# Column stores on GpSimd's queue, gates on ScalarE, and the tokens' places scattered in the last stage

## The chip, the cores and the metric

The kernel runs on one core of a Trainium2 chip. The metric is the device time of one execution in microseconds, given as the median of several runs.

## The reference

Three stages follow each other on 3072 tokens of width 512: chunked attention (8 heads, chunks of 32 with a few neighbours and 8 memory keys), a mixture of 8 experts where each token goes to the one expert with the largest logit, and a dense block with a rational activation.

```python
e_idx = np.argmax(logits, axis=1)              # one expert for each token
for e in range(E):
    mask = e_idx == e
    h = np.maximum(x[mask] @ w1[e], 0.0)       # 512 -> 1024
    out[mask] = gate_w[mask, None] * (h @ w2[e])
...
h = x @ w_in                                   # 512 -> 2048, all tokens
P = a[0] + a[1]*h + a[2]*h2 + a[3]*h3
Q = 1.0 + abs(b[0])*abs(h) + abs(b[1])*h2
return ((P / (Q + 1e-06)) @ w_out)
```

All in float32; the kernel multiplies float32 numbers as two rounded halves (high and low), which gives three products for each.

## The kernel before, in words

One program runs on the five engines, and every engine works through its own instructions in the order in which the code is written. SyncE (SP) and GpSimd (POOL) also issue DMAs, each in order on a queue of its own.

**Attention** fills the first 110 us or so, writes the rows `x` to DRAM (`xd`), and a router sorts the tokens by expert into units of 128 slots. There are 32 units (`NS`): 0 to 2 early ones, 3 to 22 in five quads of four units (`QUADS`), 23 a single last one (`S_LAST`), 24 to 29 for overflow, and 30 and 31 two small ones of at most 32 tokens. A unit's tokens belong to one expert; empty slots have an index out of bounds, which a DMA skips.

**The experts' stage** is `moe`, with the nested `quad(q)`. A quad has 8 steps `n`, of 128 hidden features each. `mm1_quad(n)` makes 12 matmuls of 512 columns (`hq`), `relu_quad(n)` cuts them on ScalarE into `hh` (line 1025) and on VectorE into `hl` (line 1026), and `mm2_quad(n - 1)` makes 12 matmuls into four accumulators (`pb`, `pa`). Behind that, `at(n)` does the work at the side:

- `filler()` is one step of the converter of the dense block's weights, which arrive as 64-bit floats: cast a piece to high and low (lines 1324, 1325; of `w_out` the halves also go out to `wod` in DRAM by GpSimd, lines 1327, 1328), load the piece after the next on SP (512 KB, line 1311, tile `wr`), and turn the bits of the next one, first on ScalarE (line 1262, which reads the loaded piece), then on VectorE (lines 1263 to 1266).
- `load_w` loads the next quad's expert weights on SP, 1 MB in a step, where the expert changes; `split_w` cuts them into high and low on ScalarE and VectorE (lines 917, 920).
- `gather` fetches the next quad's rows of `x` (four indirect DMAs of 128 rows on GpSimd, line 807), and `gate_x` multiplies each unit by its gate on GpSimd (line 907).
- `put_row(s)` scatters, for unit s, each token's number to its place in `od` (an indirect DMA on GpSimd of 128 words of 4 bytes, line 897). Quads 0 to 3 do it at every step, so unit s goes out at quad s // 8, step s % 8.

At a quad's end `put_quad` copies the four accumulators out (ScalarE and VectorE in turn) and stores them to `yd`, 256 KB each, on SP's queue (line 984). `prep_x` transposes the next quad's gathered units on TensorE (line 1081, tile `xps`): units 0 and 1 at step 7, units 2 and 3 behind the loop. Quads 0 and 3 carry a small unit as well (`mm1_small`, line 856, reads `w1r`).

Behind the last quad come the single unit's ReLU (line 1071), the turning of its hidden features (`prep_h`, lines 939 to 942), the first block's `rows.prep` (lines 1288, 1289), and its second product (line 949).

**The dense stage** is `moe2`: 6 blocks of 512 rows, 16 steps each, 24 matmuls of 512 columns a step, the second product three steps behind the first. It loads `wo` (512 KB each, from `wod`) and the next block's rows `yr` (from `yd`) on SP. `rows.load_out` reads `od` back as `out_rows` at step 4, and `evac` scatters the finished rows to the output on GpSimd (line 1472), for the first block at step 18.

Of the kernel before, what the change touches and what calls it, by code (L numbers as in the profile page):

```python
# [18 lines left out]
AF = mybir.ActivationFunctionType  # L19
ALU = mybir.AluOpType  # L20
AX = mybir.AxisListType
PSUM = bass.MemoryType.PSUM
P = 128
# [46 lines left out]
def attention(nc, tc, ex, ident, qkv, small, pos_u, out_u, start, ab):  # L70
# [8 lines left out]
    with ExitStack() as ctx:  # L79
# [190 lines left out]
        for t in range(NT):  # L270
# [13 lines left out]
            if t + NB_IN < NT + 2:  # L284
                load(t + NB_IN)
# [48 lines left out]
NS = 32  # L334
# [7 lines left out]
QUAD = 4  # L342
QUADS = 5
Q_FIRST = EARLY + 1
S_LAST = Q_FIRST + QUAD * QUADS
NC8 = 1024 // P
# [411 lines left out]
class Experts:  # L758
# [145 lines left out]

    def gate_x(self, s):
        x = self.xg[s % QUAD]
        self.nc.gpsimd.tensor_scalar(out=x, in0=x, scalar1=self.gate_s[:, s:s + 1], scalar2=None, op0=ALU.mult)

    def gate_row(self, c0, to):

# [61 lines left out]

    def put_quad(self, c0, gate=None):

        b = self.first_column(self.nc.sync, c0)
        for t in range(QUAD):
            y, ps = self.xg[(c0 + t) % QUAD], self.acc(t)
            if gate is not None:
                self.nc.vector.tensor_tensor(out=y, in0=ps, in1=gate, op=ALU.mult)
            elif t % 2 == 0:  # L980
                self.nc.scalar.copy(y, ps)
            else:
                self.nc.vector.tensor_copy(y, ps)
            self.nc.sync.dma_start(out=self.yd[t, :, bass.ds(b, QUAD * P)], in_=y)

    def clear_columns(self, zero):

# [40 lines left out]
    def acc(self, t):  # L1028
        return (*self.pb, *self.pa)[t]

    def mm2_quad(self, n):
        h, l = self.hq[n % 2]
        for t in range(QUAD):
            ps, d = self.acc(t), slice(n % 2 * 512 + t * P, n % 2 * 512 + (t + 1) * P)
            self.nc.tensor.matmul(ps, lhsT=self.w2h[:, n // 2, d], rhs=h, start=(n == 0), stop=False)
            self.nc.tensor.matmul(ps, lhsT=self.w2l[:, n // 2, d], rhs=h, start=False, stop=False)
            self.nc.tensor.matmul(ps, lhsT=self.w2h[:, n // 2, d], rhs=l, start=False, stop=(n == NC8 - 1))
# [68 lines left out]
def moe(nc, tc, ex, filler, rows, gp):  # L1106
    ET = mybir.EngineType
    flags, w1r = ex.flags, ex.w1r
    gate0 = gp.tile([P, QUAD * P], F32, name="gate0")
    small = gp.tile([P, 4, SM], F32, name="small_y")  # L1110

    def quad(q):
        c0 = Q_FIRST + QUAD * q
        nxt = range(c0 + QUAD, c0 + 2 * QUAD) if q + 1 < QUADS else range(S_LAST, S_LAST + 1)
        k = QUAD_SMALL.get(q)
        pieces = {0: (1, 0), 1: (1, 2), 2: (2, 0), 3: (2, 2)}
        loads = {n if k is None else n + 4: x for n, x in pieces.items()}
        part1, part2 = (5, 6) if k is None else (6, 7)
        sx, (sh, sT) = ex.xy[3], [x[:, 0:256] for x in ex.xg[0:2]]
        sT = sT[:, 0:P].rearrange("p (k n) -> p k n", k=4)  # L1120
        hT = ex.xg[0][:, 256:512].rearrange("p (i n) -> p i n", i=2)
        if k is not None:
            e = ex.expert(NS - 1 - k)

        def at(n):

            if n in FILLERS[q]:
                filler()
            if k is not None and n in pieces:
                layer, i = pieces[n]  # L1130
                ex.load(e, layer, range(i, i + 2))
            if n in loads:
                layer, i = loads[n]
                ex.load_w(nxt[0], layer, range(i, i + 2))
            if n == part1:
                ex.split_w(nxt[0], 1, range(2))
            if n == part2:
                ex.split_w(nxt[0], 2, range(2))
            if n == (2 if k is None else 5):
                for c in nxt:  # L1140
                    ex.gather(c)
                if len(nxt) > 1:
                    for c in nxt:
                        ex.gate_x(c)
            if q < 4:
                ex.put_row(q * NC8 + n)

        for n in range(NC8):
            ps = ex.mm1_quad(n)
            if n == 0 and q == 0:  # L1150
                ex.mm2(EARLY, 0)
                ex.put(1, ex.turn(1))
                ex.mm2(EARLY, 1)
                ex.out(EARLY)
            if n == 1 and q == 0:
                ex.put(EARLY, ex.turn(EARLY))
                ex.gate_row(Q_FIRST, gate0)
            ex.relu_quad(n, ps)
            if n == 0 and q == 0:
                ex.load_w(Q_FIRST, 2)  # L1160
                ex.split_w(Q_FIRST, 2)
            if k is not None and n == 0:
                ex.gather_small(k, sx[:, 0:D_M])
            if k is not None and n == 3:
                ex.prep_x_small(sx, sT)
            if k is not None and n == 4:
                ex.prep_h_small(sh, hT)
            if k is not None and n == 5:
                ex.put_small(k, sx[:, 0:D_M], small)
            if n == NC8 - 1:  # L1170
                xs = [(c, ex.prep_x(c, c - nxt[0] if len(nxt) > 1 else None)) for c in nxt[0:2]]
                for c, low in xs:
                    low()
            if n > 0:
                ex.mm2_quad(n - 1)
            if k is not None and n == 3:
                ex.mm1_small(sT, sh)
            if k is not None and n == 4:
                ex.out_small(k, ex.mm2_small(hT), sx)
            at(n)  # L1180
        for c in nxt[2:]:
            ex.prep_x(c, c - nxt[0])()
        ex.split_w(nxt[0], 1, range(2, 4))
        if q + 1 == QUADS:
            while filler():
                pass
            rows.open()
            for t in range(4):
                rows.load(0, t, w1r[:, t, 0:TB])
            for part in range(3):  # L1190
                ex.mm1(S_LAST, part)
        ex.mm2_quad(NC8 - 1)
        ex.put_quad(c0, gate0 if q == 0 else None)
        ex.split_w(nxt[0], 2, range(2, 4))

    def first_y(t):
        rows.prep(t, w1r[:, t, 0:TB], rows.h, rows.l)

    filler()
    ex.split_w(EARLY, 2)  # L1200
    for q in range(QUADS):
        quad(q)
    ex.hs = ex.w2r[:, 0].rearrange("p (i j n) -> p i j n", i=2, j=4)
    ex.relu(S_LAST)
    for t in range(2):
        first_y(t)
    for g in range(2):
        ex.prep_h(S_LAST, g)
    for t in range(2, 4):
        first_y(t)  # L1210
    for k in range(SMALL - 1, -1, -1):
        ex.copy_small(k)
    ALL = (ET.PE, ET.Activation, ET.DVE, ET.Pool, ET.SP)
    more = nc.values_load(flags[0:1, 2, 0:1], engines=ALL, min_val=0, max_val=1)
    tc.mark_branch_hint_location("more", "LikelyTaken", engines=(ET.PE, ET.Activation))
    for g in range(2):
        ex.mm2(S_LAST, g)
    with tc.If(more == 1, label="more"):  # L1218
        ex.clear_columns(w1r[:, 0])
        for i in range(Q_FIRST, NN):  # L1220
            if i == S_LAST or i < S_LAST and (i - Q_FIRST) % QUAD == 0:
                continue
            todo = nc.values_load(flags[0:1, 2, i:i + 1], engines=ALL, min_val=0, max_val=1)
            with tc.If(todo == 1):
                e = ex.expert(i)
                for layer in (1, 2):
                    ex.load(e, layer)
                    ex.split_w(i, layer, always=True)
                nc.gpsimd.memset(ex.xg[i % QUAD], 0.0)
                ex.gather(i)  # L1230
                ex.prep_x(i)()
                for part in range(3):
                    ex.mm1(i, part)
                ex.relu(i)
                ex.prep_h(i, 0)
                ex.prep_h(i, 1)
                for part in range(2):
                    ex.mm2(i, part)
                ex.out(i)
                ex.merge(i)  # L1240
        for t in range(4):
            rows.load(0, t, w1r[:, t, 0:TB])
        for t in range(4):
            first_y(t)
    ex.out(S_LAST, y=rows.spare, ps=ex.pb[1])
# [23 lines left out]
class Rows:  # L1269
# [10 lines left out]

    def load(self, blk, k, r):
        self.nc.sync.dma_start(out=r, in_=self.ex.yd[k, :, blk * TB:(blk + 1) * TB])

    def load_out(self):
        behind(self.tc, self.nc.sync.dma_start(out=self.out, in_=self.ex.od.rearrange("(t p) a -> p (t a)", p=P)), *self.ex.outs)
# [80 lines left out]
def moe2(nc, tc, rows, wih, wil, wod, consts, out):  # L1366
    with ExitStack() as ctx:
# [114 lines left out]
        n = len(steps)  # L1482
        for i in range(n + LAG):
            if i < n:
                mm1(*steps[i])
            if i == 1:
                rows.last(hp.tile([P, NK, P], F32, tag="h", name="yps"))
            if i == 4:
                rows.load_out()
            if 1 <= i <= n:  # L1490
                ew_act2(steps[i - 1])
# [121 lines left out]
```

## Time and profile before

| what | value |
|---|---|
| runs shown | 991.28, 993.83, 1002.33 us (median 993.83) |
| profiled execution | 995.52 us, span 994.0 us |
| PE busy | 931.9 us (94%), mean granted clock 0.974 |
| DVE, ACT, POOL busy | 747.1, 535.5, 166.1 us |
| attention, experts, dense block | about 0 to 115, 115 to 460, 460 to 994 us |

The span is the time between the first and the last instruction of the profiled execution; 1.5 us lie outside it. PE counts as busy while matmuls stream, also at half clock, so its share says where it had work and not how fast it went.

### The profile page before, as it was taken

The numbers are of one execution on the slowest core, as the hardware profiler recorded it, in microseconds if no ns is written. First come the engines' busy times: TensorE is split into PE (matmuls) and PEld (weight loads), VectorE is DVE, ScalarE is ACT, GpSimd is POOL, SyncE is SP. The second block draws the span as 40 slices with busy tenths as digits, with TensorE's granted clock in tenths as the row PEclk, the third lists the DMA queues.
The fourth block names the chain that finished last, engine by engine and source line by source line (L and its number), as shares of the span: only waits on it lengthen the run. The fifth ranks groups of instructions, "written<-read, shape, count | busy, mean of one in ns | idle before, by whom it ended". The sixth has DMA issues, their size and how long they took to land.

```text
span 994.0 us, 15359 instructions
## 1 busy us (share of the span) xinstructions
PE 931.9 (94%) x5684; PEld 752.5 (76%) x5684; DVE 747.1 (75%) x1244; ACT 535.5 (54%) x897; POOL 166.1 (17%) x194
## 2 busy tenths in 40 slices
PE   6998899797888798998999999999999999999997
PEld 5676578585667677887788888888888888888885
DVE  7677783284384725644999989998998999899885
ACT  3453433231161613324777767667776766777673
POOL 5112203074323127310000100010010001001001
PEclk9999899898889799999999999999999999999999
DMA  8998535769839365855421100010010001001001
GB/s 333 350 372 320 199 109 77 163 150 229 132 110 250 106 236 165 260 182 184 154 89 39 43 12 22 11 43 22 22 43 11 22 11 43 22 1 44 1 1 43
DMA packets 39093, 114.89 MB, mean 116 GB/s; under 512 B 8987, under 2 KB 9119, under 8 KB 36192
## 3 DMA queue, kind: packets, MB, share of 16 engines
q1 hardware_dynamic: 28800, 84.31, 29.1%
q0 software_dynamic: 9888, 28.60, 8.7%
q8 instruction: 46, 0.75, 0.3%
q10 hardware_dynamic: 320, 0.91, 0.3%
q14 instruction: 39, 0.32, 0.1%
HBM read 86.51 MB, written 27.54 MB: 115 GB/s over the span
## 4 chain that ended last, share of the span: by engine, by line
issue 57%; PE 17%; DMA 15%; POOL 5%; DVE 4%; ACT 1%; SPq 1%; POOLq 0%; ACTq 0%; DVEq 0%
DMA wod<-wo 3%; DMA wr<-in_moe_w_in 3%; DMA wr<-in_moe_w_out 2%; POOL out L1472 2%; PE pv L210 2%; DMA w1r<-in_moe_w 2%; PE pa L154 2%; PE pb L1096 1%; PE pa L949 1%; PE hq L1018 1%; PE xps L234 1%; PE hq L1019 1%; DMA out_rows<-od 1%; PE hq L1020 1%; PE pps L188 1%
## 5 line engine op out<-in xcount | busy, mean ns | idle before, releaser
L1457 PE MATMUL a<-wo,gh 128*128 128x512 f32 x384 | 149.6, 390 | 1.6 <-ACT gh L1436 1.6
L1459 PE MATMUL a<-wo,gl 128*128 128x512 f32 x384 | 149.6, 390 | 1.3 <-DVE gl L1442 1.3
L1400 PE MATMUL h<-yh,wih 128*128 128x512 f32 x384 | 149.6, 389 | 0.4 <-PEq L1218 0.4
L1402 PE MATMUL h<-yh,wil 128*128 128x512 f32 x384 | 149.4, 389 | 0.0
L1458 PE MATMUL a<-wo,gh 128*128 128x512 f32 x384 | 149.4, 389 | 0.0
L1401 PE MATMUL h<-yl,wih 128*128 128x512 f32 x384 | 149.4, 389 | 0.0
L1412 ACT ACTIVATE s<-h 128x512 f32<-128x512 f32 x96 | 56.5, 588 | 104.8 <-PE h L1402 103.0
L1472 POOL DMA_INDIRECT out<-o,out_rows x24 | 25.7, 1070 | 495.6 <-ACT o L1468 489.1
L1419 DVE SCALAR_TENSOR_TENSOR q<-s,ab,q 128x512 f32<-128x512 f32 x96 | 71.8, 748 | 40.2 <-ACT q L1413 40.2
L1459 PEld LDWEIGHTS a<-wo,gl 128*128 128x128 f32 x384 | 72.2, 188 | 17.2 <-DVE gl L1442 2.1
L1457 PEld LDWEIGHTS a<-wo,gh 128*128 128x128 f32 x384 | 72.0, 188 | 17.2 <-ACT gh L1436 2.5
L1436 ACT CAST gh<-u 128x512 fp32r<-128x512 f32 x96 | 59.9, 624 | 45.5 <-DVE u L1432 45.4
L1400 PEld LDWEIGHTS h<-yh,wih 128*128 128x128 f32 x384 | 72.1, 188 | 15.8 <-issue 0.8
L1401 PEld LDWEIGHTS h<-yl,wih 128*128 128x128 f32 x384 | 72.2, 188 | 14.9
L1458 PEld LDWEIGHTS a<-wo,gh 128*128 128x128 f32 x384 | 72.0, 187 | 15.0
L1402 PEld LDWEIGHTS h<-yh,wil 128*128 128x128 f32 x384 | 72.0, 187 | 14.9
L1414 ACT ACTIVATE u<-h,ab 128x512 f32<-128x512 f32 x96 | 74.8, 780 | 0.0
L1432 DVE SCALAR_TENSOR_TENSOR u<-u,ab,q 128x512 f32<-128x512 f32 x96 | 72.2, 752 | 3.4
L1421 DVE SCALAR_TENSOR_TENSOR u<-u,ab,h 128x512 f32<-128x512 f32 x96 | 71.8, 748 | 3.4
L1430 DVE SCALAR_TENSOR_TENSOR q<-q,ab,s 128x512 f32<-128x512 f32 x96 | 71.6, 745 | 1.7 <-ACT s L1426 1.7
L1425 ACT ACTIVATE s<-q,ab 128x512 f32<-128x512 f32 x96 | 70.2, 731 | 1.1
L1431 DVE SCALAR_TENSOR_TENSOR q<-q,s 128x512 f32<-128x512 f32 x96 | 66.4, 692 | 3.3
(307 smaller groups left out, 1817.6 us busy)
## 6 DMA issues: line engine op xcount, KB each, us to landing
in<-in_qkv SPq DMA_DIRECT2D x22, 560.0 KB
in<-in_qkv SPq DMA_DIRECT2D x22, 556.0 KB
w1r<-in_moe_w SPq DMA_DIRECT2D x20, 512.0 KB
w2r<-in_moe_w SPq DMA_DIRECT2D x20, 512.0 KB
wr<-in_moe_w_in SPq DMA_DIRECT2D x16, 512.0 KB
wr<-in_moe_w_out SPq DMA_DIRECT2D x16, 512.0 KB
wod<-wo POOLq DMA_DIRECT2D x32, 256.0 KB
wo<-wod SPq DMA_DIRECT2D x16, 512.0 KB
```

The costliest lines, as they stand in the source:

```text
L1400: nc.tensor.matmul(ps, lhsT=wih[k][:, sl], rhs=h[:, k], start=(k == 0), stop=False)
L1401: nc.tensor.matmul(ps, lhsT=wih[k][:, sl], rhs=l[:, k], start=False, stop=False)
L1402: nc.tensor.matmul(ps, lhsT=wil[k][:, sl], rhs=h[:, k], start=False, stop=(k == NK - 1))
L1414: A.activation(u, ps, func=AF.Identity, scale=a3, bias=a2)
L1419: V.scalar_tensor_tensor(out=q, in0=s, scalar=absb1, in1=q, op0=ALU.mult, op1=ALU.add)
L1421: V.scalar_tensor_tensor(out=u, in0=u, scalar=a1, in1=ps, op0=ALU.add, op1=ALU.mult)
L1425: A.activation(s, q, func=AF.Ln, bias=cb)
L1430: V.scalar_tensor_tensor(out=q, in0=q, scalar=cb, in1=s, op0=ALU.add, op1=ALU.mult)
L1432: V.scalar_tensor_tensor(out=u, in0=u, scalar=a0, in1=q, op0=ALU.add, op1=ALU.mult)
L1457: nc.tensor.matmul(ps, lhsT=gh[:, sl], rhs=wo[x][:, 0].bitcast(F32R), start=(x == 0), stop=False)
L1458: nc.tensor.matmul(ps, lhsT=gh[:, sl], rhs=wo[x][:, 1].bitcast(F32R), start=False, stop=False)
L1459: nc.tensor.matmul(ps, lhsT=gl[:, sl], rhs=wo[x][:, 0].bitcast(F32R), start=False, stop=(x == NF - 1))
```

## The change: what it does

The column stores of `put_quad` are issued by GpSimd instead of SP, with the register that holds their first column. `gate_x` is a ScalarE activation with a scale from a column instead of a GpSimd operation, and its place moves from the gather's step (2 or 5) to step 6 for units 0 and 1 and to step 7 for units 2 and 3. The 32 scatters of `put_row` leave the quads; `rows.place()` issues them together in the dense stage at step 1, behind the single unit's store, and `load_out` follows at step 14 instead of 4. The single unit's ReLU and half of its turning go in front of and between the two halves of the last quad's last `mm2_quad`, and its `rows.prep` calls follow the other half.

```diff
     def gate_x(self, s):
         x = self.xg[s % QUAD]
-        self.nc.gpsimd.tensor_scalar(out=x, in0=x, scalar1=self.gate_s[:, s:s + 1], scalar2=None, op0=ALU.mult)
+        self.nc.scalar.activation(x, x, func=AF.Copy, scale=self.gate_s[:, s:s + 1])
...
-        b = self.first_column(self.nc.sync, c0)
+        b = self.first_column(self.nc.gpsimd, c0)
...
-            self.nc.sync.dma_start(out=self.yd[t, :, bass.ds(b, QUAD * P)], in_=y)
+            self.nc.gpsimd.dma_start(out=self.yd[t, :, bass.ds(b, QUAD * P)], in_=y)
...
-    def mm2_quad(self, n):
+    def mm2_quad(self, n, ts=range(QUAD)):
...
                 for c in nxt:
                     ex.gather(c)
-                if len(nxt) > 1:
-                    for c in nxt:
-                        ex.gate_x(c)
-            if q < 4:
-                ex.put_row(q * NC8 + n)
+            if n >= NC8 - 2 and len(nxt) > 1:
+                for c in nxt[0:2] if n == NC8 - 2 else nxt[2:4]:
+                    ex.gate_x(c)
...
                 ex.mm1(S_LAST, part)
-        ex.mm2_quad(NC8 - 1)
+            ex.hs = ex.w2r[:, 0].rearrange("p (i j n) -> p i j n", i=2, j=4)
+            ex.relu(S_LAST)
+            ex.mm2_quad(NC8 - 1, range(2))
+            ex.prep_h(S_LAST, 0)
+        ex.mm2_quad(NC8 - 1, range(2, 4) if q + 1 == QUADS else range(QUAD))
...
-    ex.hs = ex.w2r[:, 0].rearrange("p (i j n) -> p i j n", i=2, j=4)
-    ex.relu(S_LAST)
-    for t in range(2):
-        first_y(t)
-    for g in range(2):
-        ex.prep_h(S_LAST, g)
-    for t in range(2, 4):
+    ex.prep_h(S_LAST, 1)
+    for t in range(4):
         first_y(t)
...
+    def place(self):
+
+        for s in range(NS):
+            self.ex.put_row(s)
...
                 rows.last(hp.tile([P, NK, P], F32, tag="h", name="yps"))
-            if i == 4:
+                rows.place()
+            if i == 14:
                 rows.load_out()
```

On GpSimd, from the end of quad 0 on, before the change (the `xy` tiles are the four units' rows, `od` the list of places, `sd` the small unit's columns):

```order
L886 DMA sd<-small_y 128x4x32
L807 DMA xy_89<-xd,src_u 128x512
L807 DMA xy_86<-xd,src_u 128x512
L834 UNCONDITIONAL_BRANCH
L807 DMA xy_87<-xd,src_u 128x512
L807 DMA xy_88<-xd,src_u 128x512
L907 TENSOR_SCALAR xy_89<-xy_89,gate_s 128x512
L907 TENSOR_SCALAR xy_86<-xy_86,gate_s 128x512
L907 TENSOR_SCALAR xy_87<-xy_87,gate_s 128x512
L834 UNCONDITIONAL_BRANCH
L907 TENSOR_SCALAR xy_88<-xy_88,gate_s 128x512
L897 DMA od<-out_u,pos_u 3072x1 x5
```

The same place on GpSimd after it:

```order
L807 DMA xy_88<-xd,src_u 128x512
L893 TENSOR_LOAD base
L893 ISA x2
L834 UNCONDITIONAL_BRANCH
L930 UNCONDITIONAL_BRANCH
L834 UNCONDITIONAL_BRANCH
L930 UNCONDITIONAL_BRANCH
L834 UNCONDITIONAL_BRANCH
L930 UNCONDITIONAL_BRANCH
L984 REGISTER_ALU
L984 DMA yd<-xy_89 128x512
L984 ISA
```

The gates and the scatters are gone from behind the gathers, and the quad's stores stand there with the load of their first column.

On ScalarE, step 7 of quad 0 before the change (`xq` holds the next quad's transposed rows, `wih` the converted weights):

```order
L1083 CAST xq<-xps 128x4x128 x2
L1324 CAST wih_2312<-wr 128x512
L1262 ACTIVATE wf<-wr 128x512
L924 TENSOR_LOAD flags
L924 ISA x2
L930 COMPARE_AND_BRANCH
L917 CAST w2h<-w2r 128x1024 x2
L930 UNCONDITIONAL_BRANCH x2
L1083 CAST xq<-xps 128x4x128
```

The same place on ScalarE after it:

```order
L1083 CAST xq<-xps 128x4x128 x2
L1326 CAST wih_2312<-wr 128x512
L1259 ACTIVATE wf<-wr 128x512
L924 TENSOR_LOAD flags
L924 ISA x2
L930 COMPARE_AND_BRANCH
L917 CAST w2h<-w2r 128x1024 x2
L930 UNCONDITIONAL_BRANCH x2
L907 ACTIVATE xy_87<-xy_87,gate_s 128x512
L834 UNCONDITIONAL_BRANCH
L907 ACTIVATE xy_88<-xy_88,gate_s 128x512
L1083 CAST xq<-xps 128x4x128 x2
```

Two gates now stand behind the converter's step and the (here skipped) cast of weights, ahead of the copies of units 2 and 3.

On ScalarE, the end of the experts' stage before the change (`w2r` holds the single unit's ReLU, `yh` the first block's rows):

```order
L981 COPY xy_89<-pb_1755 128x512
L981 COPY xy_87<-pa_80 128x512
L924 TENSOR_LOAD flags
L924 ISA x2
L930 COMPARE_AND_BRANCH
L917 CAST w2h<-w2r 128x1024 x2
L930 UNCONDITIONAL_BRANCH x2
L1071 ACTIVATE w2r<-hps 128x512 x2
L1288 CAST yh_5061<-w1r 128x512 x2
L941 CAST hh_1762<-hTp 128x512
L941 CAST hh_1764<-hTp 128x512
L1288 CAST yh_5061<-w1r 128x512 x2
```

The same place on ScalarE after it:

```order
L1071 ACTIVATE w2r<-hps 128x512 x2
L941 CAST hh_1762<-hTp 128x512
L981 COPY xy_89<-pb_1755 128x512
L981 COPY xy_87<-pa_80 128x512
L924 TENSOR_LOAD flags
L924 ISA x2
L930 COMPARE_AND_BRANCH
L917 CAST w2h<-w2r 128x1024 x2
L930 UNCONDITIONAL_BRANCH x2
L941 CAST hh_1764<-hTp 128x512
L1290 CAST yh_4965<-w1r 128x512 x4
```

The ReLU and the first half of the turning stand ahead of the accumulators' copies, and the four `yh` casts behind the second half.

## Rows read from the trace of the kernel before

**Rows 1.** Stretches, us: busy PE, PEld, DVE, ACT, POOL (count); PE clock; DMA share; GB/s.
```profile
218.90:287.60 68.70, 53.91 (x211) 42.15 (x210) 33.79 (x51) 20.29 (x32) 20.21 (x18) 0.85 0.76 138
287.60:344.90 57.30, 48.80 (x210) 39.53 (x209) 36.03 (x53) 22.70 (x35) 20.65 (x20) 0.91 0.73 193
344.90:399.60 54.70, 51.63 (x308) 41.03 (x307) 26.48 (x42) 18.38 (x34) 26.30 (x27) 0.97 0.60 204
399.60:448.80 49.20, 49.20 (x220) 40.80 (x220) 27.63 (x47) 15.33 (x26) 12.25 (x19) 1.00 0.64 209
468.00:530.00 62.00, 59.84 (x263) 48.86 (x263) 59.42 (x89) 47.31 (x78) 0.80 (x1) 1.00 0.38 127
```

**Rows 2.** PE's waits from 140 to 520 us: total us, times, longest us.
```profile
PE pb L1035 <- ACT hh L1025: 17.5, 4, 7.2
PE pb L1037 <- DVE hl L1026: 5.7, 4, 1.8
PE sps L856 <- DMA w1r<-in_moe_w: 4.6, 2, 3.3
PE xps L1081 <- POOL xy L907: 3.1, 2, 2.0
PE hTp L939 <- ACT w2r L1071: 1.3, 1, 1.3
...
PE pb L949 <- ACT hh L941: 0.9, 1, 0.9
```

**Rows 3.** Timeline of ACT: start, us, what, idle time before and its end.
```profile
238.02 0.66 ACT L1262 ACTIVATE wf<-wr 128x512 f32<-128x512 f32 x1 [11.35 <-DMA wr<-in_moe_w_in]
325.77 0.66 ACT L1262 ACTIVATE wf<-wr 128x512 f32<-128x512 f32 x1 [11.48 <-DMA wr<-in_moe_w_out]
```

**Rows 4.** Timeline of SP's queue: issue of a converter's load.
```profile
223.75 0.96 SPq L1311 DMA_DIRECT2D wr<-in_moe_w_in  x1
```

**Rows 5.** Timeline of POOL: scatters of the places.
```profile
214.43 1.07 POOL L897 DMA_INDIRECT od<-out_u,pos_u  x1 [0.17 <-issue]
...
257.32 0.97 POOL L897 DMA_INDIRECT od<-out_u,pos_u  x1 [0.30 <-issue]
...
355.78 0.98 POOL L897 DMA_INDIRECT od<-out_u,pos_u  x1 [0.30 <-issue]
```

**Rows 6.** The same view as rows 1, of stretches with slow and fast loads.
```profile
222.00:228.00 6.00, 6.00 (x28) 4.98 (x27) 4.73 (x8) 2.78 (x5) 0.00 (x0) 1.00 0.87 21
...
237.00:251.00 14.00, 10.52 (x36) 7.89 (x37) 9.38 (x15) 4.78 (x8) 10.92 (x9) 0.76 1.01 382
252.00:273.00 21.00, 16.92 (x66) 13.14 (x64) 5.03 (x9) 2.46 (x4) 5.05 (x5) 0.84 0.92 118
...
354.00:366.00 12.00, 12.00 (x79) 8.86 (x77) 1.38 (x2) 1.46 (x3) 2.15 (x3) 1.00 1.03 391
```

**Rows 7.** DMA queues from 222 to 228 us: packets, MB, share of 16 engines.
```profile
q1 hardware_dynamic: 75, 0.12, 84.6%
q0 software_dynamic: 28, 0.00, 2.8%
```

**Rows 8.** Instructions on xy and yd: duration ns min/median/max, first and last start.
```profile
L907 POOL TENSOR_SCALAR xy<-xy,gate_s x16: 1552/1568/2542, 207.0 to 393.6; 128x512 f32<-128x512 f32 x16
...
L984 SPq DMA_DIRECT2D yd<-xy x20: 3/335/447, 218.9 to 450.9; - x20
...
L971 POOL DMA_DIRECT2D yd<-xy x3: 775/817/826, 151.5 to 163.7; - x3
...
L971 POOL DMA_DIRECT2D yd<-wf x1: 798/798/798, 468.3 to 468.3; - x1
```

**Rows 9.** Timeline of ACT: an activation with a column as scale.
```profile
460.75 0.69 ACT L956 ACTIVATE wf<-pb,gate_s 128x512 f32<-128x512 f32 x1 [5.79 <-PE pb L949]
```

**Rows 10.** The chain of work that ended last: start, us, what.
```profile
465.34 9.56 DMA out_rows<-od
...
559.28 1.03 POOL out L1472
```

More of the change, by code (lines that the diff above doesn't have):

```diff
@@ L1029, in acc @@
         return (*self.pb, *self.pa)[t]
-    def mm2_quad(self, n):
+    def mm2_quad(self, n, ts=range(QUAD)):
         h, l = self.hq[n % 2]
-        for t in range(QUAD):
+        for t in ts:
             ps, d = self.acc(t), slice(n % 2 * 512 + t * P, n % 2 * 512 + (t + 1) * P)
```

## The prediction

> **What bounds the kernel now.** I read the busy times by stretch first. In the dense stage PE is all but full from its start (59.84 of 62 us, at clock 1.00 [rows 1]), and nothing in this change removes a matmul. What can be won lies in the quads. Quad 4 is the model of an undisturbed one: 49.2 us, PE busy all of it at clock 1.00 [rows 1]. It holds the quad's 192 matmuls of 512 columns and 24 more of the single unit, 216 in all, so one takes 0.228 us and a plain quad needs 43.7 us. The other quads have 16 transposes for the next units; at no more than a matmul's time each they cost at most 3.6 us, and I take 2, so the floor is 45.7 us (43.7 to 47.3). Quad 1 took 68.7 us and quad 2 57.3 us [rows 1], 23.0 and 11.6 us above it. PE's waits say why: 17.5 us for `hh` and 5.7 us for `hl` [rows 2], together 23.2 of these 34.6 us; the other 11.4 us are matmuls at the lower clock, 1.2 instead of 2.4 GHz, behind the waits (the mean granted clock of these quads is 0.85 and 0.91 [rows 1], while quad 4, without a wait, has 1.00).
>
> The wait for `hh` is not ScalarE's own work. ScalarE stood at line 1262 for 11.35 and 11.48 us until a converter's load had landed [rows 3], and the ReLU is queued behind it. The first of these loads was issued at 223.75 [rows 4] and used at 238.02, so 512 KB took 14.3 us. In fast stretches the DMA moves 382 and 391 GB/s, and 512 KB are 1.4 us of that; from 222 to 228 us it moved 21 GB/s and from 252 to 273 us 118 GB/s, at a busy share of 0.87 and 0.92 [rows 6]. So the engines were held, not idle. What runs in the slow stretches and not in the fast ones is the scatter of the places: five from 214.43 us on, about 1.3 us apart, and eight up to 257.32 us [rows 5]. The best evidence is quad 3, where the scatters (the last at 355.78 us, [rows 5]) belong to units 24 to 31, nearly all of whose indices are out of bounds: from 354 to 366 us the DMA ran at 391 GB/s [rows 6]. It is the words written that count, not the instruction. The stretch of 21 us after eight scatters (1024 words) moved 118 x 21 = 2.5 MB, which at 385 GB/s are 6.4 us, so 14.6 us were lost, some 14 ns a word.
>
> **The change, part by part.** *Scatters moved.* Quads 0 to 2 lose 24 full scatters. If loads then land in 2 to 5 us, `wr` comes a step ahead of its use, as a step is 24 x 0.228 = 5.5 us. Gain: 23.0 us in quad 1 and 11.6 us in quad 2. In quad 0 the small unit waited 4.6 us for `w1r` [rows 2]; with half clock behind it in the same proportion (11.4 to 23.2) that is 6.9 us. Sum 41.5 us. Quad 1 then has 4 MB of expert weights, 2 MB of `wr`, 1 MB of gathers and 1 MB of stores in its first four steps, 22 us: 364 GB/s, just under the 382 of rows 6. I leave 2 us for loads that are late all the same (0 to 6). At 5.5 us a step no other engine is near its limit: in quad 1 ScalarE was busy for 20.3 us and VectorE for 33.8 [rows 1], against 45.7.
>
> *Where they go.* In the dense stage GpSimd is free until the first `evac` at 559.28 us [rows 10]. They stand behind the single unit's store, issued at 468.3 us [rows 8], so 32 of them at 1.3 us end at about 511; by the 21 us for eight above, the words of the 24 full ones are in DRAM at about 469 + 24 / 8 x 21 = 532 us, and reading `od` back took 9.56 us [rows 10]: 542, 17 us ahead of its use. Hidden, as SP waits for it only at step 14, behind all loads of block 1. The other user is the loads: from 468 to 530 us the core moved 127 GB/s [rows 1], of which much is early prefetch, and beside scatters I have seen 118. So it fits barely. Cost 0 (0 to 15): the `wo` loads start with the stage, ahead of the scatters, and the last of them is needed at step 18 only.
>
> *Gates on ScalarE.* GpSimd loses 16 operations of 1.57 us [rows 8]; ScalarE gains 16 of 0.69 us [rows 9], 11 us in all over four quads. In quads 1 and 2 steps 6 and 7 have no filler, so the cover is PE's 2.7 us of `mm2_quad(6)` and enough. In quads 0 and 3 the second pair stands behind the converter's two operations: 2 x 0.66 [rows 3] and 2 x 0.69 are already these 2.7 us, and the copies of units 0 and 1 and a skipped branch come on top, partly beside the transposes. I take 0.6 us of wait in each, 1.2 together (0 to 5 with the lower clock). Against that, quad 3 loses the wait for GpSimd's gates, 3.1 us [rows 2]: without a scatter ahead of them the gathers go out 1.3 us earlier and the first gate takes 0.9 us less, so it is ready 2.2 us earlier, and the longest of the two waits was 2.0 us. But ScalarE waits for the gathers too, so I count 2 us of gain (0 to 4).
>
> *Stores on GpSimd's queue.* An issue takes 0.82 us there and 0.335 us on SP [rows 8]; 20 cost GpSimd 16 us in all. They wait for the copies out of the accumulators; behind them stand the gathers, which need the landed stores anyway, and `wod` stores. Gathers at step 2 have four steps, 22 us, until the first gate. SP's next load waits for VectorE's part of the converter, with or without stores ahead, so nothing is won there. 0 (0 to 3 lost).
>
> The Trainium skill, in "DMA: Bandwidth & Descriptors", gives simple stores to SyncE's queue (section "Issuing engine by pattern") and has GpSimd's first byte at about 1 us against 0.6 (section "Specifications"). The issues of rows 8 agree in sign (0.82 against 0.335 us). By the page the sum would lose, as an estimate, 20 x 0.4 = 8 us if nothing covered it.
>
> *The single unit.* PE waited 1.3 us for its ReLU and 0.9 us for the copy behind [rows 2]; with the lower clock in the proportion above that is 3.3 us. Now 6 matmuls (1.4 us) cover the ReLU of the half that is needed (one activation, 0.69 us [rows 9]), and 6 more the copy. Gain 3 us (1.3 to 4). The first block's `rows.prep` moves behind the turning, under 5.5 us of the unit's second product: free.
>
> **Sum** against the profiled execution of 995.5 us: 41.5 - 2 + 2 - 1.2 + 3 = 43.3, which gives 952.2. It ran 1.7 us above the median of 993.83, so 950.5 for a median; I say **950**. All good bounds together (floor 43.7, 4 and 4 gained, nothing lost) give 995.5 - 53.5 - 1.7 = 940; all bad ones but the dense stage's (floor 47.3, then 6, 5 and 3 lost, 1.3 gained) 995.5 - 25.6 - 1.7 = 968. They hardly all meet; I take 960 for this case's upper end.
>
> **Rivals.**
> *A, the contention moves along.* The scatters now come 1.3 us apart without a pause and meet `wo` and `yr`. If loads fall to a half of 118 GB/s, `yr` of block 1 lands late, ScalarE stands at its copy, and PE waits in the dense stage, where it never did: two waits of 4 to 6 us with half clock, 8 to 18 us. Speaks for it: 127 needed against 118 seen. Against: deadlines of 20 us and more. It gives 958 to 968.
>
> *B, the loads don't get faster.* The scatters' packets hold only 2.8% of the engines from 222 to 228 us, while 75 packets of the loads' queue hold 84.6% [rows 7]. If engines are shared packet by packet, the scatters can take no more than these 2.8%, and something else (HBM, the loads' own pattern) holds the loads. Then only the single unit's 3 us and 2 of quad 3 are won: 995.5 - 5 = 990.5, or 989 for a median. Against it stand the 391 GB/s of quad 3.
> The Trainium skill ("DMA: Bandwidth & Descriptors", section "Queues, rings and completion order") has each DMA engine turn between queue rows after each packet, which would be this rival; the trace's slow stretches speak against such a fair share.
>
> *C, slower: GpSimd's writes to DRAM of any size hold the loads.* Then 20 stores of 256 KB join that queue, and each quad's end gets what followed the scatters: quad 2's 11.6 us at the two ends that are free of it now (quads 3 and 4), nothing gained elsewhere, as the stores replace the scatters: 993.8 + 23.2 - 5 = 1012. It decides where loads in the 10 us behind a quad's stores fall under about 130 GB/s. Against: quad 4 has GpSimd's `wod` stores all through (19 operations on POOL in rows 1) and PE never waited.
>
> **How the numbers follow.** Forecast 0.78 (940 to 960), A 0.11, B 0.07, C 0.04. The range from 940 to 964 takes the forecast and half of A and leaves some 0.17 out. This kernel's measurement tells about 1% from no change, 10 us. Faster by over 1%: the forecast and A, 0.89; within 1%: B, 0.07; slower: C, 0.04.
>
> **What would show it.** Right: no stretch of a quad with a DMA share of 0.8 and under 130 GB/s; ScalarE's waits at the converter's bits under 3 us; quads 1 and 2 at 46 to 49 us, clock 1.00; quad 3 near 52; PE without a wait between the last quad and the dense stage; slow loads between 470 and 530 us on the old time axis, with PE at 100%. Wrong: PE waits for ScalarE or `wo` in the dense stage's first block (A); loads of 10 us and more in quads without scatters (B, C); ScalarE waiting for a gather ahead of its gates, and PE's transposes for ScalarE, for more than 2 us in a quad.

## The result, and the profile after

The changed kernel takes 953.89 us (median of 4 runs, 950.31 to 957.24), the kernel before in the same measurement 995.91 us: a ratio of 0.957, 95% interval 0.951 to 0.964. A second measurement of the same two kernels gave 951.67 against 995.41 us, 0.958 (0.954 to 0.961). The profiled execution took 950.31 us, with a span of 948.6 us at a mean clock of 0.996; it is the fastest of the four, which is why it lies 3.6 us under the median. Here and below, a ratio and its interval are those on record, taken over the undisturbed runs, and need not equal the quotient of two medians in the last digit.

The same stretches of the changed kernel as in [rows 1]: quads 1 to 4, and five us of quad 0 (start:end, length, busy PE, PEld, DVE, ACT, POOL with counts, PE clock, DMA share, GB/s).

```profile
210.00:256.10 46.10, 46.10 (x212) 38.48 (x211) 32.71 (x51) 23.59 (x36) 6.46 (x8) 1.00 0.58 205
256.10:303.70 47.60, 45.84 (x209) 37.87 (x209) 34.99 (x53) 25.20 (x39) 10.47 (x14) 1.00 0.65 232
303.70:356.20 52.50, 50.84 (x306) 40.51 (x305) 26.36 (x42) 20.97 (x38) 14.28 (x20) 0.97 0.66 223
356.20:408.00 51.80, 51.80 (x233) 42.83 (x233) 28.40 (x49) 17.17 (x30) 12.62 (x21) 1.00 0.56 188
185.00:190.00 5.00, 4.55 (x27) 3.55 (x28) 1.67 (x4) 2.58 (x6) 0.00 (x0) 0.66 0.01 2
```

PE's waits of the changed kernel from 140 to 520 us, the view of [rows 2]:

```profile
PE xps L1081 <- ACT xy L907: 3.4, 2, 1.8
PE syp L872 <- DMA w2r<-in_moe_w: 2.2, 2, 1.5
PE a L1461 <- DVE gl L1444: 1.3, 1, 1.3
PE a L1459 <- ACT gh L1438: 0.9, 1, 0.9
PE h L1402 <- ACT wf L956: 0.8, 1, 0.8
PE pb L949 <- DVE xy L983: 0.3, 1, 0.3
```

The reader is to see two things. Quad 1 is 46.1 us long and PE is busy for all of it, where [rows 1] had 53.91 of 68.7 us; and of the waits of [rows 2] for `hh`, `hl` and `w1r`, 27.8 us together, nothing is left. What is left in the quads was not among PE's waits before: two waits for ScalarE's gates (1.76 us at 295.23 in quad 2 and 1.66 us at 352.36 in quad 3) and two for the small unit's `w2r` in quad 0 (1.50 us at 184.12 and 0.68 us behind it).

The scatters now stand in the dense stage. GpSimd's timeline (start, us, what, idle time before and its end), the read of the places on SP's queue and the first use:

```profile
433.49 1.24 POOL L897 DMA_INDIRECT od<-out_u,pos_u  x1 [0.31 <-issue]
...
454.64 1.49 POOL L897 DMA_INDIRECT od<-out_u,pos_u  x1 [7.54 <-DMA od<-out_u,pos_u]
...
491.60 0.97 POOL L897 DMA_INDIRECT od<-out_u,pos_u  x1 [0.30 <-issue]
513.39 0.97 POOL L1474 DMA_INDIRECT out<-o,out_rows  x1 [20.82 <-ACT o L1470]
```

```profile
493.90 0.37 SPq L1287 DMA_DIRECT2D out_rows<-od  x1
```

And what the loads do meanwhile, in the view of [rows 1]:

```profile
435.00:440.00 5.00, 5.00 (x24) 4.14 (x23) 4.90 (x8) 3.72 (x6) 4.05 (x4) 1.00 0.59 15
440.00:445.00 5.00, 5.00 (x24) 4.14 (x23) 4.90 (x9) 3.71 (x6) 3.78 (x5) 1.00 0.79 40
460.00:465.00 5.00, 5.00 (x24) 4.14 (x23) 4.90 (x9) 3.83 (x8) 3.78 (x5) 1.00 0.50 38
475.00:480.00 5.00, 5.00 (x23) 4.13 (x23) 4.71 (x8) 4.42 (x8) 0.97 (x1) 1.00 0.86 45
433.00:494.00 61.00, 60.78 (x268) 50.38 (x269) 59.55 (x90) 45.77 (x76) 35.07 (x33) 1.00 0.73 100
```

The slow loads have not gone. They have moved to a place where PE does not need them: 15 to 45 GB/s in the slow stretches, 100 GB/s on average while the scatters last (433 to 494 us), and PE busy for 60.78 of these 61 us.

Where the 45.4 us between the two spans (994.0 and 948.6 us) came from can be read from the starts of three of PE's products (count: duration ns min/median/max, first to last start). The kernel before:

```profile
L1018 PE MATMUL hq<-xq,w1h x160: 387/389/796, 150.7 to 437.9; 128*128 128x512 f32 x160
L1096 PE MATMUL hps<-w1h,xq x16: 389/389/389, 441.9 to 445.3; 128*128 128x512 f32 x16
L1400 PE MATMUL h<-yh,wih x108: 389/389/476, 461.2 to 597.1; 128*128 128x512 f32 x108
```

The changed kernel:

```profile
L1018 PE MATMUL hq<-xq,w1h x160: 389/389/792, 146.4 to 395.3; 128*128 128x512 f32 x160
L1096 PE MATMUL hps<-w1h,xq x16: 389/389/389, 399.2 to 402.6; 128*128 128x512 f32 x16
L1402 PE MATMUL h<-yh,wih x140: 387/389/476, 415.3 to 594.7; 128*128 128x512 f32 x140
```

The first `hq` opens quad 0, the first `hps` is the single unit's, the first `h` opens the dense stage. With the stretches of the quads this gives, in us:

| part | before | after | gained | predicted |
|---|---|---|---|---|
| ahead of quad 0 | 150.7 | 146.4 | 4.3 | 0 |
| quad 0 | 68.2 | 63.6 | 4.6 | 6.9 |
| quad 1 | 68.7 | 46.1 | 22.6 | 23.0 |
| quad 2 | 57.3 | 47.6 | 9.7 | 11.6 |
| quad 3 | 54.7 | 52.5 | 2.2 | 2, less 0.6 |
| quad 4 up to the single unit | 42.3 | 43.0 | -0.7 | 0 |
| single unit | 19.3 | 16.1 | 3.2 | 3 |
| dense stage to the end | 532.8 | 533.3 | -0.5 | 0 |

The change does not touch what lies ahead of quad 0; in another profiled execution of the changed kernel the first `hq` starts at 149.3 us, so most of these 4.3 us is the spread between executions. The other parts sum to 41.1 us, against 43.3 predicted. (The column of predictions has 2.6 us more to take off, 2 for loads still late and 0.6 for a gate's wait in quad 0.)

### The profile page after: what moved, and what is told of

The parts are those of the page before. It is cut to its first block, busy times and chain, and to the rows that moved or that the text cites. A ratio compares the mean times of both kernels' runs of the same rounds, so it can differ in the third digit from the quotient of the medians.

```text
span 948.6 us, 15349 instructions
## 1 busy us (share of the span) xinstructions
PE 916.0 (97%) x5684; PEld 744.7 (79%) x5684; DVE 743.3 (78%) x1244; ACT 546.4 (58%) x913; POOL 150.9 (16%) x198
## 2 busy tenths in 40 slices
DMA packets 37814, 114.90 MB, mean 121 GB/s; under 512 B 8987, under 2 KB 9119, under 8 KB 34912
## 4 chain that ended last, share of the span: by engine, by line
issue 55%; PE 26%; POOL 7%; DMA 6%; DVE 4%; ACT 1%; POOLq 1%; ACTq 0%; DVEq 0%; SPq 0%
POOL od L897 3%; DMA yd<-xy 2%; PE pv L210 2%; PE pa L154 2%; PE hq L1018 2%; POOL out L1474 2%; PE hq L1019 2%; PE hq L1020 2%; DMA wr<-in_moe_w_out 2%; PE pps L188 1%; PE pb L1096 1%; PE pa L949 1%; PE xps L234 1%; PE pb L1035 1%; PE pb L1037 1%
```

## The experiments

Theory W is the prediction's: the words that the scatters write hold the loads, so that moving the scatters is the whole gain. The rivals are B (something else holds the loads), C (any write to DRAM from GpSimd's queue does) and the parts of the change that do not concern the scatters.

### Parts of the change, alone and undone

**e1_scatters**: only the scatters are moved.

```diff
-            if q < 4:
-                ex.put_row(q * NC8 + n)
...
                 rows.last(hp.tile([P, NK, P], F32, tag="h", name="yps"))
-            if i == 4:
+                rows.place()
+            if i == 14:
                 rows.load_out()
```

> The kernel before with one part of the change alone: the 32 scatters of the tokens' places stand in the dense stage, out_rows is read at step 14. Theory W (the words that the scatters write hold the loads of the quads): nearly the whole gain, 41.5 us less at most 6 for loads still late and 3 for the missing single-unit part, so about 955 us, 952 to 962, and the quads 1 and 2 run in 46 to 49 us each with the clock at 1.00. Theory B (something else holds the loads, and the four parts win together or by chance): 990 us, 985 to 996, with stretches of quads at a DMA share of 0.8 under 130 GB/s still there.

**e2_back**: the changed kernel with the same lines the other way round.

> The changed kernel with this part alone undone: each quad of the first four issues its eight scatters again, and out_rows is read at step 4; gates stay on ScalarE, column stores on GpSimd's queue, the single unit's ReLU early. Theory W: the loss comes back, 985 to 995 us, with loads of about 10 us again in quads 1 to 3. Theory B: 950 to 958 us, as the changed kernel.

**e3_stores**: only the column stores, and the register with their column, on GpSimd's queue.

```diff
-        b = self.first_column(self.nc.sync, c0)
+        b = self.first_column(self.nc.gpsimd, c0)
...
-            self.nc.sync.dma_start(out=self.yd[t, :, bass.ds(b, QUAD * P)], in_=y)
+            self.nc.gpsimd.dma_start(out=self.yd[t, :, bass.ds(b, QUAD * P)], in_=y)
```

> The kernel before with one part alone: the quads' column stores are issued by GpSimd. Theory W: no change within 1%, 992 to 1000 us, since SP's loads wait for the staging tiles and not for the stores ahead of them. Rival C (any write to DRAM from GpSimd's queue holds the loads): 1005 to 1020 us, with loads under 130 GB/s in the 10 us behind each quad's stores. A second rival, that SP's loads had been held up by the stores ahead of them: 970 to 985 us.

**e4_gates**: only the gates, by ScalarE at steps 6 and 7.

```diff
-        self.nc.gpsimd.tensor_scalar(out=x, in0=x, scalar1=self.gate_s[:, s:s + 1], scalar2=None, op0=ALU.mult)
+        self.nc.scalar.activation(x, x, func=AF.Copy, scale=self.gate_s[:, s:s + 1])
...
-                if len(nxt) > 1:
-                    for c in nxt:
-                        ex.gate_x(c)
+            if n >= NC8 - 2 and len(nxt) > 1:
+                for c in nxt[0:2] if n == NC8 - 2 else nxt[2:4]:
+                    ex.gate_x(c)
```

> The kernel before with one part alone: the gates are put onto x by ScalarE at steps 6 and 7. Theory W: no change within 1%, 990 to 1000 us; ScalarE's gates stand behind converter bits that wait for late loads, so PE's waits for xy may even grow by some us a quad. Rival (VectorE's and GpSimd's shared use of SBUF, or GpSimd's gates ahead of the scatters, held up the loads or the gathers): 975 to 985 us.

Measured, beside 998.71 us for the kernel before:

| kernel | median, us | ratio to before, 95% |
|---|---|---|
| e1_scatters | 952.41 | 0.953 (0.947 to 0.959) |
| e2_back | 1004.09 | 1.004 (1.000 to 1.008) |
| e3_stores | 1009.35 | 1.012 (1.009 to 1.015) |
| e4_gates | 991.36 | 0.990 (0.987 to 0.994) |

The scatters alone are the whole gain, and without their move there is none. The other three parts together make no difference that can be told from e1_scatters: the intervals overlap (0.947 to 0.959 there, 0.951 to 0.964 for the whole change).

Beside the scatters, though, stores and gates were not without effect. e2_back came back with more than was lost, 9 us over its range, and e3_stores missed its range of no change by 9 us. e4_gates fell into its range of 990 to 1000 us, though it was 7 us faster than the kernel before, which the theory had no reason for. PE's waits from 140 to 560 us of e3_stores (its three costliest are of the kinds that [rows 2] has):

```profile
PE pb L1035 <- ACT hh L1025: 25.1, 5, 9.2
PE pb L1037 <- DVE hl L1026: 10.2, 6, 2.6
PE sps L856 <- DMA w1r<-in_moe_w: 4.4, 2, 3.8
```

of e4_gates:

```profile
PE xps L1081 <- ACT xy L907: 14.0, 2, 10.1
...
PE pb L1037 <- DVE hl L1026: 5.3, 3, 1.8
PE pb L1035 <- ACT hh L1025: 4.6, 3, 1.9
```

and of e2_back:

```profile
PE xps L1081 <- ACT xy L907: 18.8, 3, 13.2
PE pb L1035 <- ACT hh L1025: 11.4, 4, 4.7
PE pb L1037 <- DVE hl L1026: 6.7, 5, 1.8
```

With gates on ScalarE the late loads are paid at another place: the gates stand behind converter bits that wait for a load, and PE's transposes stand behind the gates. That this costs 7 us less than the wait for `hh` is a measurement without a cause shown. e3_stores came out at the time that rival C gave, so C has to be looked at by its mark, slow loads behind every quad's stores. At the end of quad 3 next to no words are scattered. e3_stores issues this quad's four stores from 416.22 us on, and has in the 10 us behind them and from 400 to 450 us

```profile
416.00:426.00 10.00, 10.00 (x46) 8.29 (x45) 5.56 (x10) 4.13 (x7) 4.63 (x9) 1.00 0.88 298
400.00:450.00 50.00, 48.74 (x222) 40.14 (x221) 36.16 (x60) 19.07 (x32) 25.79 (x33) 1.00 0.71 239
```

298 GB/s where C has under 130, and the changed kernel, with all 20 stores on that queue, has no slow stretch in any quad. So C falls: the stores cost 11 us only where scatters share their queue. The trace puts the loss in quad 2, 74.0 us long instead of 57.3. There two of the quad's scatters now stand behind the stores and ahead of the gathers, and GpSimd's gates wait 11.03 us for the gathered rows. Which of these makes the loads later stays open; no run took it apart.

### What of a scatter holds the loads

Four kernels add 32 scatters to the changed kernel, where the kernel before had its own, to a scratch tensor `od2` that nothing reads. They differ in what they write.

```diff
+    def extra(self, s):
+        d = self.nc.gpsimd.indirect_dma_start(
+            out=self.od2, out_offset=bass.IndirectOffsetOnAxis(ap=self.pos_u[:, s:s + 1], axis=0), in_=self.out_u[:, s:s + 1], in_offset=None,
+            bounds_check=NT * P - 1, oob_is_err=False,
+        )
...
+            if q < 4:
+                ex.extra(q * NC8 + n)
```

This is e7_words. e6_none takes its indices from a tile of out-of-bounds numbers, e8_rows512 writes rows of `ident` (128 numbers of 4 bytes), and e9_spread multiplies the indices by 128, with an `od2` 128 times as long:

```diff
+    nc.vector.tensor_scalar(out=ex.pos_w, in0=ex.pos_u, scalar1=7, scalar2=0x3FFFFF80, op0=ALU.logical_shift_left, op1=ALU.bitwise_and)
...
-            out=self.od2, out_offset=bass.IndirectOffsetOnAxis(ap=self.pos_u[:, s:s + 1], axis=0), in_=self.out_u[:, s:s + 1], in_offset=None,
-            bounds_check=NT * P - 1, oob_is_err=False,
+            out=self.od2, out_offset=bass.IndirectOffsetOnAxis(ap=self.pos_w[:, s:s + 1], axis=0), in_=self.out_u[:, s:s + 1], in_offset=None,
+            bounds_check=(NT * P - 1) * P, oob_is_err=False,
```

> The changed kernel plus 32 extra scatters in the quads, where the kernel before had its own, to a scratch tensor that nothing reads; every index is out of bounds, so that the instruction runs on GpSimd and no word is written. Theory W (the written words hold the loads): within 1% of the changed kernel, 948 to 958 us. Rival I (the instruction itself, its 1.3 to 1.6 us on GpSimd's queue with descriptors made for each row, holds the loads): most of the 41.5 us comes back, 980 to 1000 us.

> The changed kernel plus 32 extra scatters in the quads, each writing 4-byte words with the real indices (neighbouring places) to a scratch tensor that nothing reads. Theory W: 35 to 40 us more than the changed kernel, 985 to 998 us, with loads of some 10 us in quads 1 to 3. Rival B (it was not the words): 950 to 960 us. If the kernel with empty scatters has lost as much, it is the instruction and not the words.

> The changed kernel plus 32 extra scatters in the quads, each writing rows of 512 bytes (128 times the bytes) with the real indices to a scratch tensor that nothing reads. If the price is one per written piece whatever its size, or more with bytes: 985 us or more. If the price comes from pieces that are smaller than what DRAM takes at once: about 950 to 962 us, since 64 KB for a scatter are a fraction of the 2 MB that a quad loads.

> The changed kernel plus 32 extra scatters in the quads, each writing 4-byte words to a scratch tensor that nothing reads, with the real indices times 128, so that the words lie 512 bytes apart instead of side by side. If the price comes from many engines writing into the same few hundred bytes: about 950 to 962 us. If it is a price for each small word wherever it lies: 985 to 998 us, as with neighbouring words.

Measured, beside 998.01 us for the kernel before:

| kernel | what a partition's index writes | median, us | ratio to before, 95% |
|---|---|---|---|
| e6_none | nothing | 955.29 | 0.959 (0.953 to 0.966) |
| e7_words | 4 bytes, side by side | 1003.15 | 1.006 (1.002 to 1.010) |
| e8_rows512 | 512 bytes, side by side | 956.30 | 0.958 (0.951 to 0.965) |
| e9_spread | 4 bytes, 512 bytes apart | 955.29 | 0.959 (0.952 to 0.966) |

e7_words against e6_none settles the instruction against the words: 47.9 us for the same 32 instructions. (That is 8 us more than the range of 35 to 40 expected. e7_words, like e2_back and e3_stores, has the column stores and the scatters on one queue, and its quad 2 is as long as theirs, 74.3 us; so a part of the 47.9 may be this surplus.) But e9_spread was the surprise. The same number of words of the same size, 512 bytes apart, costs nothing that shows. The price is not one of small words; it is one of small words beside each other. Nor is it one of packets (a packet is one piece of a transfer in the profile's list): e6_none, e7_words and e9_spread all have 10011 packets under 512 bytes, 32 for each added scatter more than the 8987 of the changed kernel.

The stretch of quad 1 with the scatters shows it, in the view of [rows 1]. e7_words:

```profile
218.00:236.00 18.00, 15.79 (x70) 12.75 (x68) 5.75 (x11) 3.86 (x7) 8.04 (x10) 1.00 0.97 132
```

e9_spread, of which the second stretch has six scatters of 128 words:

```profile
216.00:234.00 18.00, 18.00 (x81) 14.92 (x80) 11.29 (x19) 6.50 (x11) 13.36 (x13) 1.00 0.89 316
225.00:235.00 10.00, 10.00 (x46) 8.26 (x44) 5.22 (x9) 2.65 (x5) 6.19 (x7) 1.00 1.02 382
```

The queues of e9_spread from 225 to 235 us (packets, MB, share of 16 engines) answer to [rows 7]; q1 is the loads' queue, q0 GpSimd's, which here carries gathers too:

```profile
q1 hardware_dynamic: 994, 3.04, 78.3%
q0 software_dynamic: 371, 0.76, 22.7%
```

The loads' queue of the kernel before in the whole stretch from 252 to 273 us:

```profile
q1 hardware_dynamic: 934, 2.46, 90.3%
```

In [rows 7] the loads' queue had 75 packets in 6 us, which held 84.6% of 16 engines: 0.846 x 16 x 6 / 75 = 1.08 us for a packet on average. In e9_spread it is 0.783 x 16 x 10 / 994 = 0.126 us, for packets nearly twice as large (3.06 KB against 1.6 KB). From 252 to 273 us it is 0.903 x 16 x 21 / 934 = 0.325 us. So neighbouring words make the loads' packets longer, some eight times in the worst stretch and two to three times over a longer one, while the scatters' own packets hold the engines for 2.8% of the time [rows 7]. It is an average: the trace's list of single packets shows some held for microseconds and the others at their usual length. Of the loads' 2 KB packets from 252 to 273 us the median took 0.084 us and the longest 5.39 us; in e9_spread from 225 to 235 us the median was 0.084 us too, and the longest 0.296 us.

### How far apart, and a kernel that follows from it

**e11_64B** is e9_spread with a shift by 4 instead of 7, so that the words lie 64 bytes apart. **e12_before_spread** is the kernel before with nothing moved: its own scatters stay where they are, and `od` gets places 512 bytes apart, by the same shift of the indices (`pos_w`) as in e9_spread.

```diff
-            out=self.od, out_offset=bass.IndirectOffsetOnAxis(ap=self.pos_u[:, s:s + 1], axis=0), in_=self.out_u[:, s:s + 1], in_offset=None,
-            bounds_check=NT * P - 1, oob_is_err=False,
+            out=self.od, out_offset=bass.IndirectOffsetOnAxis(ap=self.pos_w[:, s:s + 1], axis=0), in_=self.out_u[:, s:s + 1], in_offset=None,
+            bounds_check=(NT * P - 1) * P, oob_is_err=False,
...
-        behind(self.tc, self.nc.sync.dma_start(out=self.out, in_=self.ex.od.rearrange("(t p) a -> p (t a)", p=P)), *self.ex.outs)
+        behind(self.tc, self.nc.sync.dma_start(out=self.out, in_=self.ex.od.rearrange("(t p r) a -> p t (r a)", p=P, r=P)[:, :, 0]), *self.ex.outs)
```

> The changed kernel plus 32 extra scatters in the quads, each writing 4-byte words to a scratch tensor that nothing reads, with the real indices times 16, so that the words lie 64 bytes apart. Theory N (what costs is that the words lie side by side): if the neighbourhood that costs is 64 bytes or less, 950 to 962 us, as with 512 bytes; if it is larger, in proportion to the words that still share one, 965 to 1000 us. Theory W (each small word costs), which the words 512 bytes apart speak against: 985 us or more.

> The kernel before with nothing moved: its own 32 scatters stay in the quads, ahead of everything they stood ahead of, but the places in od lie 512 bytes apart, and out_rows is read with that step. Theory N: nearly the whole gain without a move, 950 to 962 us, clock 1.00 in quads 1 and 2, no load of 10 us behind the scatters. Theory W (words as such, or the place of the scatters in GpSimd's queue): 985 to 1000 us, as the kernel before.

Beside 994.36 us for the kernel before, e11_64B took 956.65 us, 0.961 (0.955 to 0.968), and e12_before_spread 955.87 us, 0.960 (0.953 to 0.966). Words 64 bytes apart are as free as words 512 bytes apart; distances between 4 and 64 bytes were not tried. Spreading the words also spreads the whole tensor, from 12 KB to 196 KB at 64 bytes; whether the distance between two words or the size of the region counts was not taken apart. e12_before_spread has eight scatters from 230.69 to 239.92 us, in quad 1, as the kernel before has from 247.95 to 257.32, and its loads run beside them:

```profile
230.00:241.00 11.00, 11.00 (x50) 9.09 (x49) 8.20 (x15) 4.26 (x7) 8.71 (x9) 1.00 0.92 310
```

In [rows 6] the stretch behind these scatters ran at 118 GB/s. So nearly the whole gain of this change, 38.5 us where the change won 42.0 and 43.7, with intervals that overlap, is to be had by one shift of the indices, with every other instruction left in its place. Reading `od` back with a step took 10.62 us there, against 9.56 us [rows 10].

### The gates earlier

**e13_gates** is the changed kernel with the gates ahead of the converter, and in quads without a small unit at step 5, ahead of the next weights' casts. **a2_after** is the changed kernel again, for the comparison.

```diff
+            if len(nxt) > 1:
+                for c in nxt if (k is None, n) == (True, 5) else nxt[0:2] if (k is None, n) == (False, 6) else nxt[2:4] if (k is None, n) == (False, 7) else ():
+                    ex.gate_x(c)
             if n in FILLERS[q]:
...
-            if n >= NC8 - 2 and len(nxt) > 1:
-                for c in nxt[0:2] if n == NC8 - 2 else nxt[2:4]:
-                    ex.gate_x(c)
```

> The changed kernel once more, word for word, as the measure for the next one: 948 to 958 us.

> The changed kernel with ScalarE's gates earlier: all four at step 5, ahead of the converter and of the casts of the next weights, in quads without a small unit; at steps 6 and 7, ahead of the converter, in the two with one. Theory: the two waits of PE for gates (1.76 and 1.66 us, in quads 2 and 3) go, with the 1.7 us that the half clock costs behind the second: 3 to 5 us less than the changed kernel, 945 to 955 us. Rival (ScalarE then waits for the gathers, with the ReLU and the casts behind it): the same or up to 5 us more.

a2_after took 951.67 us, 0.958 (0.954 to 0.961) of the kernel before, and e13_gates 950.08 us, 0.956 (0.953 to 0.960): 1.6 us less, with intervals that overlap, so not told apart. PE's waits of e13_gates from 140 to 520 us:

```profile
PE hq L1019 <- DVEq L930: 2.5, 2, 2.3
PE syp L872 <- DMA w2r<-in_moe_w: 2.2, 2, 1.5
```

Both waits for gates are gone, as the theory had it, and one of 2.3 us has come in their place. Its rows, on PE and on VectorE:

```profile
356.88 0.50 PE L1019 MATMUL hq<-xq,w1h 128*128 128x512 f32 x1 [2.30 <-DVEq L930]
```

```profile
354.35 0.69 DVE L1263 SCALAR_TENSOR_TENSOR wr<-wr,wf 128x512 int32<-128x512 int32 x1
355.53 1.29 DVE L1085 TENSOR_TENSOR xq<-xps,xq 128x512 fp32r<-128x512 f32 x2 [0.49 <-DVEq L930]
```

PE's transposes come earlier, but VectorE takes the low parts of the next x (`xq`, line 1085) only behind its converter, and these end at 356.82 us. The wait moved from ScalarE to VectorE.

## Why the prediction was right, point by point

**What bounds the kernel.** Right: the late loads were the path. The floor of 45.7 us (43.7 to 47.3) for a plain quad holds; quads 1 and 2 took 46.1 and 47.6 us at clock 1.00.

**Scatters moved.** The mechanism, late loads behind the scattered words, and the sum were right (quads 0 to 2 gained 36.9 of the predicted 41.5, less 2, us). One reading was loose: what runs in the slow stretches is not the scatters' issue. From 222 to 228 us GpSimd issues none [rows 6], and the first of the eight was issued at 247.95 us, inside the stretch called fast. The loads slow down some us behind the issues. One size was off: quad 0 gained 4.6 us for 6.9. I took the small unit's wait for `w1r` as gone, with its clock, and nothing as late next; the next late thing was the same unit's `w2r`, 2.2 us of waits and five us at a clock of 0.66 behind them. It is there in all kernels without the slow loads (2.1 us in e1_scatters, 2.3 in e12_before_spread), so it is not the scatters'.

**"It is the words written that count, not the instruction."** Right as far as it went (e6_none), and half of the truth: the prediction's price of 14 ns a word holds for words side by side alone. It was read from one kind of scatter, and no row of the kernel before could have told the two apart. That the forecast came out all the same is luck in one respect: the words kept their neighbours and went to a stage that has the time, so the difference between neighbouring and spread words never came into play.

**Where they go.** Right, and close: 32 scatters and their words were to take 63 us from the first issue (469 to 532), and took 60.4 (433.49 to 493.90, when `od` is read); they were to be ready 17 us ahead of their use, and were ready 15.8 us ahead (the read took 3.73 us, from 493.90, against 513.39). Not as predicted, GpSimd itself waited for earlier scatters, 7.54 us at the longest, so that the last issue came 58 us after the first and not 42. The dense stage lost 0.5 us. Rival A is out: the loads fell to 15 to 45 GB/s, far under the half of 118 that it took, for some us at a time, but the mean beside the scatters was 100, and PE waited for no load.

**Gates on ScalarE.** The place and the size were off: 3.4 us of PE's waits instead of 1.2, in quads 2 and 3 instead of 0 and 3. In quad 2 I had named the cover, PE's 2.7 us of `mm2_quad(6)`, and only the gates to hide under it. The chain was longer: a converter's load came 3.01 us late, and two casts of `w1h` and two of `w2h`, 2.00 and 1.98 us, stood between it and the first gate. ScalarE's timeline:

```profile
288.97 0.67 ACT L1259 ACTIVATE wf<-wr 128x512 f32<-128x512 f32 x1 [3.01 <-DMA wr<-in_moe_w_out]
290.18 2.00 ACT L917 CAST w1h<-w1r 128x1024 fp32r<-128x1024 f32 x2 [0.54 <-issue]
...
292.58 1.98 ACT L917 CAST w2h<-w2r 128x1024 fp32r<-128x1024 f32 x2
294.46 1.33 ACT L907 ACTIVATE xy<-xy,gate_s 128x512 f32<-128x512 f32 x2
```

**Stores on GpSimd's queue.** 0 with the scatters gone, as predicted; 11 us beside them, which the prediction did not ask since the two go together. An issue took 0.54 us there, not 0.82. That is the time of an issue and not the time to the first byte, beside which the prediction set it; the latter was not measured.

**The single unit.** 3.2 us for 3, but only about half of it by the new order. e1_scatters keeps the old order and PE's two waits of 1.3 and 0.9 us, and its single unit takes 17.8 us at a clock of 1.00, where the kernel before took 19.3 us at 0.91. So the order gained 1.7 us and the clock 1.5 us; the prediction put both down to the order. Why the clock fell behind the same waits in one kernel and not in the other is not shown.

**Rival B** fell by the slow stretches that went to the dense stage with the scatters, and by e7_words. Its argument was the scatters' small share of the engines' time [rows 7]; the queue rows above show the flaw, that a share counts who holds an engine, not who makes the holder slow. The Trainium skill ("DMA: Bandwidth & Descriptors", section "Queues, rings and completion order") has each DMA engine turn between queues after each packet; the runs do not speak against that. But such turns set no bound to the loss here, as it was the loads' own packets that took 1.08 us on average instead of 0.126.

Of the marks named ahead, two were missed by little: ScalarE's waits at the converter's bits reach 3.4 us instead of staying under 3, and 1.1 us of PE's waits are left between the last quad and the dense stage.

## What to carry to other kernels

Where loads are slow while the DMA engines look busy, compare the mean time of a packet of the slow queue in a slow and in a fast stretch, and look for what else was written just before, however few bytes it is. In these runs scattered 4-byte words cost the other queues dearly when they landed side by side and nothing measurable when they landed 64 bytes apart, so try places that far apart before planning where in the program the scatter may stand. And when an engine's wait is moved away, follow its whole queue to the next late thing: here `w2r` behind `w1r`, and VectorE's `xq` behind ScalarE's gates.

## What the runs showed of the hardware that I had not expected

- Behind scatters of 4-byte words side by side, another queue's packets took 1.08 us on average (1.6 KB each), against 0.126 us (3.06 KB each) beside the same words 512 bytes apart. Whether the memory or the engines are held is not shown.
- 512-byte rows side by side, 128 times the bytes, cost no measurable time (956.30 against 955.29 us without any write).
- PE's wait of 1.66 us at 352.36 us was followed by a clock of 0.83 in the stretch from 350 to 360 us; the one of 1.76 us at 295.23 left it at 1.00 from 290 to 300 us.
